# Fifty-four instead of fifty-one pairs of max tiles in front of the loop of a gated attention and token-mixing kernel

## The chip, the core and the metric

The kernel runs on one core of a Trainium2 chip, as one program. The metric is the device time of one execution in microseconds; the median of several runs counts. In the text TensorE multiplies matrices, VectorE and ScalarE work on rows of 128 partitions, GpSimd does elementwise work in on-chip memory, and SyncE issues DMAs.

## The reference

The input x has 2048 tokens of 640 channels. One branch is attention with 32 heads of 20 channels, all of which share one key and one value head; the other is a mixer that applies a two-layer network across the tokens. A sigmoid gate of each token mixes the two.

```python
g = _sigmoid((x * gate_w).sum(-1, keepdims=True))
q = (x @ wq).reshape(B, S, H, Dh); k = x @ wk; v = x @ wv        # S = 2048, H = 32, Dh = 20
p = _softmax(einsum("bhqd,bkd->bhqk", q, k) * Dh ** -0.5)
a = einsum("bhqk,bkd->bhqd", p, v).reshape(B, S, H * Dh) @ wo
h = _layernorm(x)
u = _gelu(einsum("bsd,sf->bdf", h, w1) + b1)                     # F = 1728
y = einsum("bdf,fs->bds", u, w2) + b2
return g * a + (1 - g) * y.transpose(0, 2, 1)
```

## The kernel before

**Units.** Attention is cut into 32 units: four blocks of 512 queries by eight groups of four heads. A unit has 16 key blocks of 128, and in all there are 512 visits (unit, key block). A visit computes four score tiles of 128 keys by 512 queries (`qk`, L685, matmul in L689), ScalarE takes their exponentials (L701), and `pv_mm` (L721, matmul in L724) multiplies them by the values.

**Max tiles.** The softmax needs the largest score of each query before its first exponential. For that every unit has 64 max tiles of its own: a matmul of 128 queries by 512 keys (L507) and a maximum over the row on VectorE (L515). The array is used as two halves of 64 rows, and each half has 32 of the unit's 64 tiles. `ms_next(b)` (L493) gives the next tile of half b, in order through the units; `given[b]` counts those given, so the unit of a half's next tile is `given[b] // 32`. When both halves of a unit are complete, `ms_done` (L524) reduces, negates and splits the maxima; `store_max` and `fetch_max` carry them by DMA into extra rows of the unit's q tile, where the score matmul subtracts them.

**In front of the loop** (L608 to L650) the first ten of 28 blocks of the mixer's first product are computed, 160 steps of six matmuls each (L634). Between steps, `lead()` (L616) issues one pair of max tiles, one in each half of the array; the two run side by side. `LEAD` says how many pairs there are, spread evenly from the fourth step to six before the last (L636). Their results rotate over four banks.

**The loop** (L1240) has 248 stretches, eight to a unit. A stretch has four visits' score tiles of one half of the array, a share of max tiles, and filler matmuls: 72 stretches have 24 of the mixer's first product (L1012), then 128 have 20 or 21 of its second (L839), then 48 have 15 of the attention's output projection (L965). `wants` (L1221) says how many max tiles a stretch gets: 6 in the first two, 10 in the other stretches of the first product, 8 in those of the second. What is left of the 2048 is spread over the output projection's stretches but the last three, in rising order (L1227, L1228). `arrange` (L1158) puts a stretch's instructions in order by a cost table written into the kernel. A last part of eight longer stretches without max tiles ends the program.

**Bursts.** Behind each stretch `burst` (L1189) multiplies the exponentials of an earlier pair of visits by the values: eight products, which follow one another without other matmuls between. If the next stretch's share reaches a unit n whose q tile has been requested, the burst also takes over the waits for q tile n's loads, one on each of its first six products:

```python
        if len(wants) > us[1] // 2 + 2:
            counts = share(us[1] // 2 + 2)
            n = max((given[b] + counts[b] - 1) // 32 for b in range(2))
            if n in qtiles:
                arrived.extend(q_loads.pop(n, ()))
```

**Loads of q.** `new_q(n)` asks for the q tile of unit n as six DMAs of 80 KB from DRAM (L148). Five tiles are alive at a time. It is called behind stretches 8u + 7 (L1252 to L1256): for units 3 and 4 behind stretch 7, 5 and 6 behind stretch 15, and from there on one a unit, u + 5 behind the last stretch of unit u. A load waits until the tile that it overwrites has been read for the last time. SyncE issues all DMAs in program order.

Of the kernel before, what the change touches and what calls it, by code (L numbers as in the profile page):

```python
# [27 lines left out]
NQ = H // 4  # L28
NU = NQB * NQ
PRO = 10  # L30
LEAD = 51
TAIL = 16
FIFTH = (4, 9, 14, 19, 24)
EPS = 1e-5
# [5 lines left out]
def mix_kernel(ctx: ExitStack, tc: tile.TileContext, A_x, A_wq, A_wk, A_wv, A_wo,  # L40
# [567 lines left out]
    with tc.tile_pool(name="psb", bufs=2, space=PSUM, side="right") as psb, \  # L608
# [13 lines left out]
        for fc in range(PRO):  # L622
            pu = [psb.tile([P, NB], F32, name=f"pu{r}") for r in range(2)]
            for hf in range(4):
# [4 lines left out]
                for c in range(HS):  # L629
                    st = hf * HS + c  # L630
                    for k, (w, h) in enumerate(((wh, h_hi[0]), (wh, h_lo[0]), (wl, h_hi[0]))):
                        for r in range(2):
                            rows = slice(64 * r, 64 * r + 64)
                            nc.tensor.matmul(pu[r][:, :HD2], w[rows, c, :], h[rows, st, :],  # L634
                                             start=(st == 0 and k == 0), stop=(st == NS - 1 and k == 2))
                    done = [max(0, min(x, last) - skip) * LEAD // (last - skip) for x in (at, at + 1)]  # L636
                    if done[1] > done[0]:
# [833 lines left out]
```

## Time and profile before

| | |
|---|---|
| median of 3 runs | 1613.25 us (1612.93 to 1613.55) |
| profiled execution | 1613.6 us |
| its span, first to last instruction | 1611.7 us |
| TensorE busy | 1603.9 us |
| VectorE busy | 1378.1 us |
| ScalarE busy | 1262.4 us |
| GpSimd busy | 844.7 us |

A row of the profile names the engine, the line of the kernel and the operation, then the tile that is written and those that are read, the shape, how many there are, and how long one takes. PE stands for TensorE's matmuls, PEld for its weight loads, DVE for VectorE, ACT for ScalarE, POOL for GpSimd, SP for SyncE; a q behind the name stands for the engine's sequencer, which issues DMAs and waits. In a row of the timeline the first number is the start in microseconds from the start of the span and the second the time that the merged group of instructions took; idle time and what ended it stand in brackets. A row of windows has the stretch, its length, the busy time and count of each engine, the granted clock of TensorE, the DMA engines' busy share and the rate in GB/s. A row of waits has the total, the number and the longest in microseconds.

The stage of projections ends at about 96 us, the ten blocks in front of the loop at 179 us; the loop's first product runs until about 614 us, the second until about 1330, the output projection until about 1545.

### The profile page before, as it was taken

The page shows a single profiled execution, that of the slowest core. Times are in us where ns is not written, and L with a number is a line of the kernel's source. Part 1 is how long each engine was busy: PE and PEld are TensorE (multiplying, and loading weights), DVE is VectorE, ACT ScalarE, POOL GpSimd, SP SyncE. Part 2 cuts the span into 40 slices and gives each one's busy share as a digit, 9 for nine tenths or more (in the row PEclk, how much of TensorE's full clock was granted, in tenths as well). Part 3 has the DMA queues.
Part 4 walks back from the last instruction along what each step waited for, and adds up shares of the span by engine and source line. Part 5 has one row for each costly group of instructions (what it writes and reads, how often), then busy time and mean ns, then how long its engine had stood idle before and what let it go on. Part 6 is the DMA issues. An engine that isn't in the chain of part 4 may idle for free.

```text
span 1611.7 us, 39437 instructions
## 1 busy us (share of the span) xinstructions
PE 1603.9 (100%) x14865; PEld 1118.7 (69%) x14865; DVE 1378.1 (86%) x2622; ACT 1262.4 (78%) x2353; POOL 844.7 (52%) x930
## 2 busy tenths in 40 slices
PE   9999999999999999999999999999999999999998
PEld 7899866766767766666666666666666666666665
DVE  6689899999999999888888998888888986667743
ACT  4445677777777778888888888888888889999996
POOL 6567767777787776544554344444444433333340
PEclk9999999999999999999999999999999999999999
DMA  7665322222222122222212121122221113322341
GB/s 216 204 170 140 92 60 75 61 75 76 69 69 76 48 75 63 81 69 69 64 52 59 36 63 57 53 60 61 61 61 47 41 48 102 116 83 82 90 137 57
DMA packets 180437, 129.53 MB, mean 80 GB/s; under 512 B 41617, under 2 KB 150062, under 8 KB 180246
## 3 DMA queue, kind: packets, MB, share of 16 engines
q1 hardware_dynamic: 179958, 126.68, 27.9%
q8 instruction: 117, 1.92, 0.5%
q14 instruction: 74, 0.61, 0.1%
q10 hardware_dynamic: 288, 0.33, 0.1%
HBM read 93.57 MB, written 32.15 MB: 78 GB/s over the span
## 4 chain that ended last, share of the span: by engine, by line
PE 99%; ACT 1%; POOL 0%; DVE 0%; issue 0%; DVEq 0%; POOLq 0%
PE xs L724 30%; PE xs L689 18%; PE xs L507 18%; PE g L839 11%; PE g L1012 7%; PE pp L303 4%; PE pu L634 4%; PE g L965 3%; PE x L507 1%; PE xs L919 1%; PE pp L367 0%; ACT p L701 0%; PE pt L295 0%; PE xs L1436 0%; PE pp L192 0%; PE g L919 0%
## 5 line engine op out<-in xcount | busy, mean ns | idle before, releaser
L515 DVE TENSOR_REDUCE mp<-xs 128x1 f32<-128x512 f32 x1946 | 1198.0, 685 | 146.4 <-PE xs L507 74.8
L701 ACT ACTIVATE p<-xs 128x512 f32<-128x512 f32 (+1 forms) x1840 | 1013.9, 678 | 4.0 <-PE xs L689 2.9
L746 POOL TENSOR_TENSOR osum<-osum,part 128x512 f32<-128x512 f32 x216 | 279.2, 1293 | 615.5 <-ACT part L745 599.1
L724 PE MATMUL xs<-p,v_sb 128*32 128x512 f32 x4096 | 492.3, 598 | 0.0
L689 PE MATMUL xs<-q,kst 62*128 62x512 f32 x1344 | 477.0, 418 | 1.3 <-ACT p L701 1.3
L507 PE MATMUL xs<-kst,q 60*128 60x512 f32 x1242 | 432.8, 415 | 0.0
L689 PEld LDWEIGHTS xs<-q,kst 62*128 62x128 f32 x1344 | 236.6, 185 | 74.8 <-DVE mp L515 53.9
L745 ACT ACTIVATE part<-xs 128x512 f32<-128x512 f32 x216 | 130.0, 602 | 199.7 <-PE xs L724 198.4
L1012 PE MATMUL g<-slot,w 64*128 64x320 f32 x1728 | 266.8, 306 | 0.0
L724 PEld LDWEIGHTS xs<-p,v_sb 128*32 128x32 f32 x4096 | 107.0, 109 | 226.6 <-issue 157.7
L1012 PEld LDWEIGHTS g<-slot,w 64*128 64x128 f32 x1728 | 259.0, 184 | 1.9
L507 PEld LDWEIGHTS xs<-kst,q 60*128 60x128 f32 x1242 | 207.1, 184 | 72.6 <-DVE mp L515 52.0
L127 POOL TENSOR_TENSOR w<-wr,w 128x512 fp32r<-128x512 f32 (+1 forms) x180 | 225.2, 1252 | 34.8 <-ACT w L124 22.7
L689 PE MATMUL xs<-slot,kst 62*128 62x512 f32 x568 | 206.2, 417 | 0.3 <-ACT p L701 0.3
L507 PE MATMUL xs<-kst,slot 60*128 60x512 f32 x576 | 204.4, 418 | 0.0
L839 PE MATMUL g<-u,w 64*128 64x320 f32 x1296 | 201.8, 306 | 0.0
L839 PE MATMUL g<-slot,w 64*128 64x320 f32 x1296 | 201.3, 306 | 0.0
L839 PEld LDWEIGHTS g<-u,w 64*128 64x128 f32 x1296 | 195.7, 184 | 1.5
L839 PEld LDWEIGHTS g<-slot,w 64*128 64x128 f32 x1296 | 195.5, 184 | 1.7
L689 PEld LDWEIGHTS xs<-slot,kst 62*128 62x128 f32 x568 | 99.6, 185 | 30.5 <-DVE mp L515 21.8
L507 PEld LDWEIGHTS xs<-kst,slot 60*128 60x128 f32 x576 | 95.1, 185 | 33.5 <-DVE mp L515 25.2
L965 PE MATMUL g<-slot 64*128 64x320 f32 x720 | 118.2, 306 | 0.0
(189 smaller groups left out, 1448.8 us busy)
## 6 DMA issues: line engine op xcount, KB each, us to landing
wr<-in_B_w_dram SPq DMA_DIRECT2D x155, 256.0 KB
q<-q_scr SPq DMA_DIRECT2D x126, 80.0 KB
rb<-r_scr SPq DMA_DIRECT2D x120, 64.0 KB
slot<-o_scr SPq DMA_DIRECT2D x24, 320.0 KB
y_scr<-yo SPq DMA_DIRECT2D x16, 320.0 KB
q_scr<-qh SPq DMA_DIRECT2D x19, 256.0 KB
q_scr<-ql SPq DMA_DIRECT2D x19, 256.0 KB
o_scr<-rb SPq DMA_DIRECT2D x120, 40.0 KB
```

Of the source, the lines that this page charges most:

```text
L127: nc.gpsimd.tensor_sub(wl, wr, f32(wh))
L303: nc.tensor.matmul(pp, w, t, start=first and n == 0, stop=not more and n == len(steps) - 1)
L507: mm = nc.tensor.matmul(ms, qtiles[n][64 * b:64 * b + 60, pr, qt * P:(qt + 1) * P], kst[64 * b:64 * b + 60, kq * NB:(kq + 1) * NB], start= ...
L515: red = nc.vector.tensor_reduce(out, ms, axis=AX.X, op=ALU.max)
L689: mm = nc.tensor.matmul(s, kst[64 * b:64 * b + 62, kb * P:(kb + 1) * P], q[64 * b:64 * b + 62, pr, :], start=True, stop=True)
L701: act = nc.scalar.activation(p_all[:, a * NB:(j + 1) * NB], s, AF.Exp, scale=SCALE)
L724: mm = nc.tensor.matmul(o[32 * hh:32 * hh + 32, :], v_sb[:, units[u][1], :], p_all[:, j * NB:(j + 1) * NB], start=first, stop=last, skip_g ...
L745: touch(nc.scalar.activation(part, o, AF.Copy), [("x", i)])
L746: nc.gpsimd.tensor_add(osum[n], osum[n], part)
L839: other_tile(half, nc.tensor.matmul(hold["p"][:, :HD2], w[r, fc % HS, :], u[d][r, fc, :], start=(hold["n"] == 1), stop=(hold["n"] == 6 * F ...
L965: other_tile(half, nc.tensor.matmul(hold["p"][:, :HD2], o[r, c, :], w[r, c, d * HD2:(d + 1) * HD2], start=(hold["n"] == 1), stop=(hold["n" ...
L1012: other_tile(half, nc.tensor.matmul(hold["p"][:, :HD2], w[r, st % HS, :], h[d][r, st, :], start=(hold["n"] == 1), stop=(hold["n"] == 6 * NS)))
```

## The change

`LEAD` goes from 51 to 54. `lead()` is called three times more in the same 160 steps, so six max tiles more are done when the loop starts. `wants` gives the output projection's stretches what is left: 204 tiles and not 210. Of its 45 stretches with max tiles, 15 had four and 30 had five; now 21 have four and 24 have five. The share of every other stretch is as before in number; which tiles it holds shifts by three in each half.

```diff
 PRO = 10
-LEAD = 51
+LEAD = 54
 TAIL = 16
```

## The prediction

> **What bounds the kernel now.** I read the page first, then the stages in windows, then single stretches in order of time.
>
> ```profile
> PE 1603.9 (100%) x14865; PEld 1118.7 (69%) x14865; DVE 1378.1 (86%) x2622; ACT 1262.4 (78%) x2353; POOL 844.7 (52%) x930
> ...
> PE 99%; ACT 1%; POOL 0%; DVE 0%; issue 0%; DVEq 0%; POOLq 0%
> ```
>
> ```profile
> core 0: us, PE busy (x) PEld busy (x) DVE busy (x) ACT busy (x) POOL busy (x), PEclk, DMA share, GB/s
> 96.40:179.00 82.60, 82.60 (x1063) 80.27 (x1062) 77.14 (x138) 38.55 (x73) 60.43 (x52) 1.00 0.56 151
> ...
> 189.26:552.64 363.38, 363.38 (x3482) 257.26 (x3481) 361.84 (x684) 286.05 (x527) 258.85 (x306) 1.00 0.26 68
> ...
> 1334.52:1399.31 64.79, 64.79 (x603) 40.37 (x603) 39.62 (x82) 63.22 (x128) 19.77 (x19) 1.00 0.35 105
> 1404.18:1524.93 120.75, 120.75 (x1102) 75.26 (x1101) 85.05 (x171) 112.84 (x226) 40.13 (x38) 1.00 0.30 89
> ```
>
> TensorE has work in every microsecond of every stage, and the chain that ended last runs through it for 99%. So whatever adds TensorE time, or holds up TensorE's queue, lengthens the kernel by that much, unless the engine finds the time again later. The four windows are: the stage in front of the loop; sixty stretches of the first product in the loop; fourteen stretches of the output projection with four max tiles each; twenty-five with five each. In the second window VectorE is busy 361.84 of 363.38 us: there two engines are full at once, and time lost by both can't be found again.
>
> **The three added pairs.** In the stage in front of the loop a pair follows every third step (18 matmuls of L634), now and then every second (12).
>
> ```profile
> 123.96 0.39 PE L507 MATMUL x<-kst,q 60*128 60x512 f32 x2
> 124.19 1.49 PE L634 MATMUL pu<-slot,w 64*128 64x320 f32 x18
> 125.51 0.39 PE L507 MATMUL x<-kst,q 60*128 60x512 f32 x1
> ...
> 174.94 0.39 PE L507 MATMUL x<-kst,q 60*128 60x512 f32 x1
> 175.17 1.05 PE L634 MATMUL pu<-slot,w 64*128 64x320 f32 x12
> 176.06 0.39 PE L507 MATMUL x<-kst,q 60*128 60x512 f32 x2
> ...
> 121.28 1.29 DVE L515 TENSOR_REDUCE mp<-x 128x1 f32<-128x512 f32 x2 [0.27 <-PE x L507]
> ```
>
> From pair to pair it is 125.51 - 123.96 = 1.55 us over three steps and 176.06 - 174.94 = 1.12 us over two. One step is then 0.43 us, and a pair 1.55 - 1.29 = 0.25 us; from the start of a pair to the next L634 it is 124.19 - 123.96 = 0.23. Three pairs cost 3 x 0.235 = **+0.70 us**. Does VectorE follow? Two maxima take 1.29 us with an overlap of 0.09 (one is 0.69), so 1.20 a pair, six tiles 3.6 us more. The 82.60 us window has 77.14 us of it in use, 80.7 after, while the window itself grows to 83.3. There is room, though little, and four banks let the engine lag by a pair; I add nothing. If that cover were gone the price would be bounded by the 3.6 us. The last six pairs stand at the same steps in both kernels, so the passage into the loop is as it was.
>
> **The six tiles that go.** They leave six stretches of the output projection, which change from five max tiles to four. Both kinds are in the trace: 64.79 / 14 = 4.628 us with four and 120.75 / 25 = 4.830 with five. So 6 x 0.202 = **-1.21 us**. Two tiles in front of the loop share one pass of 0.235 us, one each row half; here a tile pays 0.202 alone. That is the whole planned gain: 0.5 us.
>
> **What moves with it.** Between the two places every max tile is computed three tiles per row half earlier, and so is the first use of each unit's q tile, while the loads of q stay where they are: after the stretch in which the unit that held the buffer ends. A burst of products (L724) takes a wait for all six pieces of q(n) if the next stretch's share reaches unit n (L1193). For unit 3: a half has given 51 tiles at the loop's start, then 6 in the first two stretches and 30 in the next six, 87 at the end of stretch 7. Stretch 8 gives its own half 8 more, 95 in all; unit 3 begins with tile 97. So the wait stands a stretch later, in the burst after stretch 8. With 54 the sums are 90 and 98: the wait moves into the burst after stretch 7, and that is the very stretch whose end releases the buffer for q3.
>
> ```profile
> 219.53 1.92 PE L724 MATMUL xs<-p,v_sb 128*32 128x512 f32 x16
> ...
> 225.60 1.92 PE L724 MATMUL xs<-p,v_sb 128*32 128x512 f32 x16
> ...
> 231.67 1.92 PE L724 MATMUL xs<-p,v_sb 128*32 128x512 f32 x16
> ```
>
> ```profile
> SPq L148 <- PE xs L507: 4.5, 1, 4.5
> ```
>
> ```profile
> 224.66 2.21 SPq L148 DMA_DIRECT2D q<-q_scr  x6
> 226.91 2.24 SPq L148 DMA_DIRECT2D w<-q_scr  x6
> ```
>
> ```profile
> 229.27 0.40 SPq L103 DMA_DIRECT2D wr<-in_B_w_dram  x1
> ...
> 229.78 0.44 SPq L103 DMA_DIRECT2D wr<-in_B_w_dram  x1
> ```
>
> ```profile
> L724 PE MATMUL xs<-p,v_sb x20: 592/592/617, 225.6 to 231.7; 128*32 128x512 f32 x20
> ...
> L724 PEldq EVENT_SEMAPHORE  x1: 51/51/51, 231.2 to 231.2; - x1
> ```
>
> The burst after stretch 7 starts at 225.60, the one after stretch 8 at 231.67; the wait stands before the latter (231.2). SyncE had stood 4.5 us for TensorE before it could issue q3, from 224.66 on. When does q3 land? The trace has no row for it, so it is bounded. The issues rotate over eight semaphores, and each waits for the one eight before it: the weight load at 229.27 is eight behind q3's fifth piece, the one at 229.78 eight behind the sixth. So the last piece lands shortly before 229.78; I take 229.7. Today that is 2 us ahead of 231.67 and free. After the change the burst at 225.60 needs it. Its eight products go in two groups of four; the waits hang on the first six, one each, so the sixth, in the second group, waits longest. The second group starts half of (1.92 - 0.59) + 0.22 = 0.89 us into the burst (592 ns is the median of one L724 matmul), at 226.49. The stall is 229.8 - 226.5 = 3.3 us if the first five products slip through while the others wait, and 229.8 - 225.6 = 4.2 if nothing does. One wait alone stands as an instruction of its own (x1), so the others hang on the products themselves, which is nearer to the lower end; I take **+3.5 us**. Behind the waiting product stand the rest of the burst and the whole of stretch 8; VectorE and ScalarE run dry behind it. It isn't found again, since in this stage VectorE has 1.54 us to spare in sixty stretches.
>
> The sixteen loads of units 13 to 28 have their wait one stretch earlier too, in the burst one stretch behind the load's release instead of two. The two tightest by their rows:
>
> ```profile
> 1015.88 2.46 SPq L148 DMA_DIRECT2D q<-q_scr  x6
> ```
>
> ```profile
> 1016.21 1.92 PE L724 MATMUL xs<-p,v_sb 128*32 128x512 f32 x16
> 1021.78 0.64 PE L724 MATMUL xs<-p,v_sb 128*32 128x512 f32 x4
> ```
>
> ```profile
> 1284.55 3.30 SPq L148 DMA_DIRECT2D q<-q_scr  x6
> ```
>
> ```profile
> 1284.86 1.92 PE L724 MATMUL xs<-p,v_sb 128*32 128x512 f32 x16
> 1290.43 1.06 PE L724 MATMUL xs<-p,v_sb 128*32 128x512 f32 x8
> ```
>
> q3's six issues end at 226.87 and its last piece is there by 229.78, 2.9 us later. By the same 2.9 us the later of these two lands at 1287.85 + 2.9 = 1290.8, and the sixth product would come at 1290.43 + 0.89 = 1291.3: 0.5 us to spare. The other lands at 1018.34 + 2.9 = 1021.2 and has until 1022.7: 1.4 us. Between 0 and 0.5 us in all; I take **+0.2**. The row maxima of some units (L537, its split and its store) come a stretch or two earlier, in the same number and beside the same work: nothing.
>
> **Sum.** 0.70 - 1.21 + 3.5 + 0.2 = +3.2 us. The profiled execution took 1613.6 us (span 1611.7, 1.9 around it), 0.35 over the median; 1616.8 for it, so 1616.4 for the median of 1613.25. With the stall from 3.3 to 4.2, the late loads from 0 to 0.5, and half a microsecond off the low end for a last piece that lands well before 229.78, this case by itself spans 1615.6 to 1617.4. A measurement of this kernel can tell some 0.2%, 3.2 us, from no change: the forecast stands right on that edge.
>
> **Rivals.** *The wait costs nothing* (not slower). If q3's pieces were there when the sixth product comes, 0.70 - 1.21 = -0.5 us would be left: 1612.7. For it: the tile itself is read only by the last two max tiles of stretch 8. Against it: the wait is put in front of the burst, and the load can't leave before 224.66, 1.8 us ahead of 226.49, while its issue alone takes 2.21. It decides from a landing before 226.5. 0.07.
>
> *The later loads are late too.* If in eight of them the last piece lands 0.8 us later than I reckon, each stalls 0.3: +2.4 us, 1618.8. For it: 0.5 us of slack at the tightest, and DMA traffic that differs from load to load (2.46 against 3.30 us for the issues alone). Against: the second tightest has 1.4 us by the same reckoning, and all their surroundings shift along. 0.12.
>
> *TensorE's clock falls in the stall.* At the start the clock was half for a while:
>
> ```profile
> 1.45 2.93 PE L192 MATMUL pp<-kst 128*128 128x512 f32 x6 [1.45 <-DVE kst L65]
> 4.17 1.05 PE L295 MATMUL pt<-ident,xa 128*128 128x128 f32 x4
> ...
> 7.33 0.60 PE L295 MATMUL pt<-ident,xa 128*128 128x128 f32 x4
> ```
>
> ```profile
> 186.83 0.49 PE L689 MATMUL xs<-q,kst 62*128 62x512 f32 x1 [0.95 <-ACT p L701]
> ```
>
> Four transposes took 1.05 us at 4.17 and 0.60 at 7.33, so up to 5.9 us of matmuls ran slowly from the first one. The longest pause I found behind that is 0.95 us, with the granted clock at 1.00 in every window above. A stall of 3.5 us is longer; half a clock for 2 to 5.9 us costs 1.0 to 2.9 us, 2.3 as a middle: 1618.7. Against it: TensorE isn't empty all that time, since the first piece, issued 1.9 us before the sixth, lets its product go at about 227.8, which leaves a pause of some 2.2 us behind the 225.6 at which stretch 7 ends. 0.07. [...]
>
> *It doesn't do what it says* can be left aside, since the counts are constants of the program; 0.04 stands for a gain of over 3.2 us from something that I don't see.
>
> **How the numbers follow.** The forecast has 0.70; just under half of it, 0.32, lies above 1616.5. Slower by over 0.2%: 0.32 + 0.12 + 0.07 = 0.51. Within 0.2%: 0.38 + 0.07 = 0.45. Faster: 0.04. The range from 1615.2 to 1619.0 holds the forecast's span, both slower rivals' times, and a margin below; it leaves out the free wait, the gain, and late loads of more than 2.6 us, about 0.2 together.
>
> **What would show it.** In the profile of the changed kernel: the stage in front of the loop 0.7 us longer with pairs at the same pitch; a burst at about 226.3 whose L724 rows spread over 5.3 us and not 1.92, with TensorE idle there until a DMA of q; the burst behind it at about 235.9 and not 231.67; then the same rhythm from burst to burst (6.06, later 5.57 us) with the offset kept; six more stretches of 4.63 us in the output projection. If the offset of about 4.2 us behind stretch 8 is missing, or shrinks before the output projection, the forecast is wrong in that step; if it grows in the middle of the loop, the later loads are late.

## The result and the profile after

| | before | after |
|---|---|---|
| median of 18 runs each, same chip | 1613.26 us (1612.89 to 1614.25) | 1615.84 us (1615.38 to 1616.83) |
| profiled execution, span | 1613.6, 1611.7 us | 1616.83, 1615.0 us |

The change costs 2.58 us; the ratio is 1.0016 with a 95% interval from 1.001 to 1.0022. The profiled execution is the highest of the 18 runs of after, 0.99 us above the median. Most of that lies ahead of any changed code: the first L634 starts at 97.25 us and in before at 96.35; in the experiments' profiles between 95.79 and 96.84. So I compare times between marks inside the kernel, and not the spans.

The page of after first: the engines' busy time, and the chain that ended last.

```profile
PE 1606.8 (99%) x14865; PEld 1119.4 (69%) x14865; DVE 1377.9 (85%) x2622; ACT 1261.8 (78%) x2353; POOL 846.4 (52%) x930
...
PE 97%; DMA 1%; ACT 1%; DVE 0%; SPq 0%; POOL 0%; issue 0%; DVEq 0%
```

The counts are those of before, as they must be, and TensorE is still the chain. In the loop one place stands out. The timelines of TensorE, VectorE and SyncE in after, around the end of stretch 7 (start, duration; in brackets the idle time before and its inferred cause):

```profile
225.87 0.48 PE L507 MATMUL xs<-kst,q 60*128 60x512 f32 x2
227.73 3.93 PE L724 MATMUL xs<-p,v_sb 128*32 128x512 f32 x16 [1.38 <-ACT yo L561]
231.59 0.50 PE L689 MATMUL xs<-q,kst 62*128 62x512 f32 x1
...
235.77 0.64 PE L724 MATMUL xs<-p,v_sb 128*32 128x512 f32 x4
```

```profile
227.44 1.28 DVE L515 TENSOR_REDUCE mp<-xs 128x1 f32<-128x512 f32 x2
232.16 4.89 DVE L515 TENSOR_REDUCE mp<-xs 128x1 f32<-128x512 f32 x8 [3.43 <-PE xs L689]
```

```profile
225.36 2.20 SPq L148 DMA_DIRECT2D q<-q_scr  x6
227.61 2.39 SPq L148 DMA_DIRECT2D w<-q_scr  x6
```

The burst's rows take 3.93 us and not 1.92, behind a pause of 1.38: 1.38 + 3.93 - 1.92 = 3.39 us lost, and VectorE stands empty for 3.43 behind it. Beware of the bracket: it puts the pause down to ScalarE's L561. That is the last event ahead of the burst and not what it waited for: in before the same burst starts at 225.60 and that L561 only at 226.48. The loads of q3 are being issued from 225.36 to 227.56. By the semaphore events in the trace of after the first piece has landed at 227.59 and the sixth at 230.19, and each of the first six products starts 0.04 to 0.14 us behind its piece, the first at 227.73. The second experiment (wait51) puts the same wait in front of the same burst of before, and its timeline names the load for a pause inside the burst.

The stages in the order of time, from the profiled executions; each entry is the time from the mark before it to this one (a burst is its first L724, counted from 1 at the loop's start):

| up to | before | after | difference |
|---|---|---|---|
| first L634 | 96.35 | 97.25 | +0.90 |
| first L689 (stage in front of the loop) | 82.70 | 83.29 | +0.59 |
| burst 1 (the first two stretches) | 10.21 | 9.44 | -0.77 |
| burst 6 | 30.28 | 30.26 | -0.02 |
| burst 8 (the stall) | 12.14 | 15.54 | +3.40 |
| burst 72 (first product) | 387.16 | 387.63 | +0.47 |
| burst 200 (second product) | 715.69 | 715.71 | +0.02 |
| burst 214 | 64.79 | 64.76 | -0.03 |
| burst 221 (six changed stretches and one unchanged) | 33.83 | 32.59 | -1.24 |
| burst 244 | 111.08 | 111.50 | +0.42 |
| end | 67.50 | 67.08 | -0.42 |

Without the start and the last two rows, which move by as much between profiles of kernels with the same number of pairs (burst 221 to 244 took 111.05 to 111.40 us with 51 and 111.12 to 111.56 with 54; the end 66.9 to 67.5 in all of these), the sum is +2.42 us, against 2.58 between the medians.

### The profile page after: what moved, and what is told of

It is laid out like the page before. It is cut to its first block, busy times and chain, and to the rows that moved or that the text cites. A ratio compares the mean times of both kernels' runs of the same rounds, so it can differ in the third digit from the quotient of the medians.

```text
span 1615.0 us, 39430 instructions
## 1 busy us (share of the span) xinstructions
PE 1606.8 (99%) x14865; PEld 1119.4 (69%) x14865; DVE 1377.9 (85%) x2622; ACT 1261.8 (78%) x2353; POOL 846.4 (52%) x930
## 3 DMA queue, kind: packets, MB, share of 16 engines
q8 instruction: 117, 1.92, 0.5%
## 4 chain that ended last, share of the span: by engine, by line
PE 97%; DMA 1%; ACT 1%; DVE 0%; SPq 0%; POOL 0%; issue 0%; DVEq 0%
PE xs L724 30%; PE xs L689 18%; PE xs L507 17%; PE g L839 11%; PE g L1012 7%; PE pu L634 4%; PE pp L303 3%; PE g L965 3%; PE x L507 1%; PE xs L919 1%; ACT p L701 1%; PE pp L367 0%; PE pt L295 0%; DMA xa<-in_A_x_dram 0%; DMA xb<-in_A_x_dram 0%; SPq L188 0%
## 5 line engine op out<-in xcount | busy, mean ns | idle before, releaser
L515 DVE TENSOR_REDUCE mp<-xs 128x1 f32<-128x512 f32 x1940 | 1194.5, 684 | 151.5 <-PE xs L689 82.7
L724 PE MATMUL xs<-p,v_sb 128*32 128x512 f32 x4096 | 494.2, 598 | 1.4 <-ACT yo L561 1.4
L689 PE MATMUL xs<-q,kst 62*128 62x512 f32 x1344 | 476.4, 417 | 0.4 <-ACT p L701 0.3
L689 PEld LDWEIGHTS xs<-q,kst 62*128 62x128 f32 x1344 | 236.8, 185 | 73.1 <-DVE mp L515 51.1
L724 PEld LDWEIGHTS xs<-p,v_sb 128*32 128x32 f32 x4096 | 107.6, 109 | 229.4 <-issue 157.2
L127 POOL TENSOR_TENSOR w<-wr,w 128x512 fp32r<-128x512 f32 (+1 forms) x180 | 226.8, 1262 | 33.3 <-ACT w L124 15.5
L689 PE MATMUL xs<-slot,kst 62*128 62x512 f32 x568 | 205.9, 417 | 0.2 <-ACT p L701 0.2
L689 PEld LDWEIGHTS xs<-slot,kst 62*128 62x128 f32 x568 | 99.8, 185 | 30.8 <-DVE mp L515 21.8
```

The source lines that it names most:

```text
L127: nc.gpsimd.tensor_sub(wl, wr, f32(wh))
L515: red = nc.vector.tensor_reduce(out, ms, axis=AX.X, op=ALU.max)
L689: mm = nc.tensor.matmul(s, kst[64 * b:64 * b + 62, kb * P:(kb + 1) * P], q[64 * b:64 * b + 62, pr, :], start=True, stop=True)
L724: mm = nc.tensor.matmul(o[32 * hh:32 * hh + 32, :], v_sb[:, units[u][1], :], p_all[:, j * NB:(j + 1) * NB], start=first, stop=last, skip_g ...
```

## The experiments

The theory: the wait for q3, moved into the burst after stretch 7, costs 3.4 us, and without it the change would be 0.8 us faster than before. The rival: the loss grows with the number of pairs, without a step. The kernels are named by what they do and by their number of pairs. The first four ran beside before at 1613.36 us, the last four at 1613.22.

**lead52 and lead53: fewer pairs.** With 52 the wait stays where it was in before, with 53 it moves.

```diff
-LEAD = 51
+LEAD = 52        # lead53: 53
```

> LEAD 52. By the wait theory (the loss is one stall at the burst behind stretch 7, and it begins at the count where unit 3 comes into stretch 8's share) nothing is lost here, since the sums are 88 and 96 and unit 3 begins with tile 97: one pair costs 0.235 us, two tiles less in the output projection give 0.40, so 1613.1 us, within 0.8 of it for what the first two stretches do. By the rival (each added pair costs its own time somewhere, 2.58 us over three pairs) it is 0.86 us slower, 1614.1.

> LEAD 53. By the wait theory the sums are 89 and 97, the wait moves into the burst behind stretch 7, and the whole stall of 3.4 us is there at once: 1613.25 + 0.47 - 0.81 + 3.4 = 1616.3 us, or 1615.5 if the first two stretches are 0.8 us shorter as with 54; the burst behind stretch 7 takes 3.9 us. By the rival, two pairs cost two thirds of the loss: 1615.0 us, with no step between 52 and 53.

Measured: 1613.9 us (1.0003, 0.9994 to 1.0012) and 1615.46 (1.0013, 1.0005 to 1.0022). The step of 1.6 us lies between 52 and 53. The rows of the burst after stretch 7, TensorE's timeline, first with 52 pairs and then with 53:

```profile
226.35 1.92 PE L724 MATMUL xs<-p,v_sb 128*32 128x512 f32 x16
```

```profile
226.83 3.60 PE L724 MATMUL xs<-p,v_sb 128*32 128x512 f32 x16 [1.30 <-ACT yo L561]
```

With 52 the burst is the one of before; with 53 it loses 1.30 + 3.60 - 1.92 = 2.98 us (3.04 from burst to burst). lead52 settles less than I wanted: its time lies between what the theory and the rival gave, nearer to the rival's, and half a microsecond over before, though no stall is in its trace. 0.29 of it is found below, under the row maxima. The medians' step is also only half of the stall. Between the marks of the table lead53 has 0.34 us less than lead52 up to burst 72 and 0.37 less up to burst 221; another 0.7 lies behind burst 221, in stretches that are the same in both, and was not followed up. So the two traces tell the theory from the rival here, and the medians alone do not.

**wait51: the wait alone.** Before with its 51 pairs, but the burst behind stretch 7 takes over q3's waits.

```diff
                 n = max((given[b] + counts[b] - 1) // 32 for b in range(2))
+                if us == (12, 13):
+                    n = 3
                 if n in qtiles:
```

> LEAD 51 as before, and the waits for unit 3's q tile put by hand into the burst behind stretch 7. No max tile moves. By the wait theory it loses the stall alone: 1613.25 + 3.4 = 1616.7 us. By the rival nothing changes: 1613.3 us.

Measured: 1616.93 us (1.0022, 1.0013 to 1.003), 3.57 over before. TensorE's timeline:

```profile
226.83 2.06 PE L724 MATMUL xs<-p,v_sb 128*32 128x512 f32 x6 [1.35 <-ACT yo L561]
229.18 1.94 PE L724 MATMUL xs<-p,v_sb 128*32 128x512 f32 x10 [0.29 <-DMA q<-q_scr]
```

The 16 rows are eight products of two rows each. Three products (six rows) start as their pieces land; then comes a pause, for which the profile does name the load of q, and then the rest. The first pause is put down to L561 here too, in a kernel where only the wait differs from before. From burst to burst it is 7.48 + 8.42 - 12.14 = 3.76 us. Why the same wait cost 3.04 us in lead53, 3.40 in after and 3.76 here was not followed up.

**free54: the change without the moved wait.** After, where the burst doesn't take over q3's waits; the two max tiles at the end of stretch 8 that read q3 carry them.

```diff
-                if n in qtiles:
+                if n in qtiles and n != 3:
```

> LEAD 54, and the burst no longer takes over the waits for unit 3's q tile; they stay with the matmuls that read it, the last max tiles of stretch 8 (about 3 us into the stretch, 5 us behind the burst's start, when the load has landed). By the wait theory the 3.4 us come back: 1615.84 - 3.4 = 1612.4 us, 0.8 us faster than before. By the rival it stays near 1615.8.

Measured: 1612.21 us (0.9994, 0.9985 to 1.0003), 3.6 under after, with both stretches back at 6.07. Adding the wait to before costs 3.57, taking it from after gives 3.63: that is shown from both sides.

**lead55 and ask55: one pair more.** With 55 the waits of fifteen later loads move into the burst right behind the stretch that releases the buffer, as that of q3 did with 53; ask55 has the same 55 pairs, but no burst takes over any wait for a load.

```diff
-LEAD = 51
+LEAD = 55
...
-                arrived.extend(q_loads.pop(n, ()))
+                q_loads.pop(n, ())      # ask55 alone
```

> LEAD 55. By the wait theory the counts decide: with 55 the waits of units 13 to 28 come one burst earlier again, into the burst right behind the stretch that releases the buffer, as unit 3's did with 53. By the landings in the profile with 54 (last piece 3.0 to 5.6 us behind that burst's start, unit 14's ahead of it), fifteen of them stall 2.2 to 4.9 us each, 55 us together: about 1671 us, 1655 to 1675. By the rival (a cost of each pair) it is 1616.7 us.

> LEAD 55, and no burst takes over the waits for a q tile; each stays with the max tile that reads it first. By the wait theory that reader stands at the end of the next stretch, some 4.9 us behind the burst's start, where the pieces have landed or lack up to 0.8 us: 0 to 6 us left of the 55, so 1612 to 1618 us. If the price lay in the loads themselves or in the traffic that they meet, it would stay near lead55's time.

Measured: 1670.06 us (1.0362, 1.0343 to 1.038; four runs from 1665.49 to 1675.84) and 1612.61 (0.9995, 0.9986 to 1.0004). In the waits of lead55 TensorE's bursts (L724) stand for loads 15 times, in those of ask55 not once; the answer has the total, the number and the longest:

```profile
PE xs L724 <- DMA q<-q_scr: 20.9, 10, 2.6
PE xs L724 <- DMA slot<-q_scr: 5.8, 5, 1.5
```

So 57 us hang on where the wait stands and not on the loads: the tiles that read them come late enough that hardly any time is lost there. The pauses named are 26.7 us. From burst to burst lead55 is 54 us behind ask55 in their profiles: behind the pauses the products come apart as in the burst after stretch 7 (four of these bursts, at 711.42, 856.49, 1096.53 and 1193.02, take 4.28, 3.37, 4.77 and 4.23 us and not 1.92), and the granted clock was 0.50 in three stretches of 3.41 us (last section). How thin the margin is that the prediction put at 0.5 us for the tightest late load, lead55 doesn't tell, since it moves the waits by a whole stretch, some 5.6 us. The semaphore events of after do: the tightest of the sixteen landed 5.64 us behind the start of the burst at 1289.47, and the product that needs it comes 5.58 + 0.88 = 6.46 behind that, which leaves 0.8 us.

**cast51 and cast54: the entry into the loop.** The first two stretches of after are 0.77 us shorter, which I had not foreseen. Before and after, ScalarE's and GpSimd's timelines, GpSimd's rows first and ScalarE's second in each:

```profile
184.38 0.46 POOL L583 TENSOR_SCALAR yo<-yo 128x320 f32<-128x320 f32 x1
184.92 0.87 POOL L584 TENSOR_TENSOR yo<-yo 128x320 f32<-128x320 f32 x1
...
185.82 0.47 ACT L571 ACTIVATE yo<-yo 128x320 f32<-128x320 f32 x1 [1.25 <-POOL yo L584]
```

```profile
185.09 0.46 POOL L583 TENSOR_SCALAR yo<-yo 128x320 f32<-128x320 f32 x1
185.63 0.87 POOL L584 TENSOR_TENSOR yo<-yo 128x320 f32<-128x320 f32 x1
...
186.54 0.47 ACT L571 ACTIVATE yo<-yo 128x320 f32<-128x320 f32 x1 [0.35 <-POOL yo L584]
```

GpSimd's share of the gelu starts at the same distance from the first L634 (184.38 - 96.35 = 88.03, 185.09 - 97.25 = 87.84), because four weight splits (L126, L127) stand ahead of it. ScalarE's tanh waits for it, the exponentials stand behind the tanh in ScalarE's queue, and TensorE waits for those: the 0.95 us at 186.83, which the prediction quotes. If this is right, time that TensorE spends in front of the loop is hidden behind GpSimd, and GpSimd relieved of part of its splits gives the same gain without any pairs. In all eight kernels with these splits on GpSimd the first burst comes 4.88 to 4.90 us behind the start of L583, and L583 starts 87.84 to 88.45 us behind the first L634, in no order of the pairs. lead53 shows the hiding too: there TensorE waits 0.89 us for a max tile (L515) in front of the first L689, so the stage is 1.40 longer than in before, and the entry 1.21 shorter. cast51 is before with the high halves of four more chunks of weights cast by ScalarE; cast54 is free54 with the same.

```diff
-            if c < 4 * PRO:
+            if c < 4 * PRO + 4:
                 nc.scalar.activation(wh, wr, AF.Copy)
```

> LEAD 51, the last four weight chunks that are split ahead of the loop get their high half from ScalarE (as the ones before them do) and not from GpSimd. Theory: the entry into the loop waits for GpSimd, whose splits delay its part of the last gelu, behind which ScalarE's exponentials queue; the added pairs gave GpSimd time, so their 0.7 us was paid back there. Then this kernel's first two stretches take 9.4 us and not 10.2, and it runs 0.8 us faster: 1612.5. Rival: the 0.8 us come from the banks in which the last pair lies, or by chance; then it stays at 1613.3.

> LEAD 54 with the wait of unit 3's q tile left to its readers (as free54, 1612.2 us) and ScalarE's casts as in cast51. By the theory on GpSimd there is nothing left to gain at the entry: 1612.2 us, first two stretches at 9.4 as in free54, and the three pairs now show at 0.7 us against cast51. By the rival it equals free54 too, but cast51 stays 1.1 us above it instead of 0.3.

Measured: 1612.02 us (0.9991, 0.9982 to 0.9999) and 1611.89 (0.9992, 0.9983 to 1.0001). The entry in windows, from the first L689 to the first burst: before, after, cast51, cast54.

```profile
179.05:189.26 10.21, 8.91 (x79) 7.44 (x77) 7.29 (x13) 8.28 (x16) 9.13 (x12) 1.00 0.37 98
```

```profile
180.53:189.97 9.44, 9.02 (x80) 7.40 (x76) 7.29 (x13) 8.27 (x16) 8.36 (x11) 1.00 0.32 86
```

```profile
178.72:188.10 9.38, 8.73 (x78) 7.42 (x76) 7.12 (x13) 8.68 (x17) 7.30 (x9) 1.00 0.39 109
```

```profile
179.38:188.86 9.48, 8.83 (x80) 7.31 (x77) 7.13 (x13) 8.68 (x17) 6.75 (x9) 1.00 0.31 86
```

And in cast51 ScalarE's tanh has no wait in front of it any more:

```profile
184.62 0.52 ACT L571 ACTIVATE yo<-yo 128x320 f32<-128x320 f32 x1
```

With GpSimd out of the way the entry takes 9.4 us with 51 pairs, and three pairs more now cost what the prediction gave them: from cast51 to cast54 the stage and the entry grow by 0.62 + 0.10 = 0.72 us. The row maxima (see below) add 0.40 and the output projection takes off 1.21, so 0.1 us should be gained, and the medians differ by 0.13. cast54 has the lowest median, 1.3 us under before and 3.95 under after, but only 0.13 under cast51, and its interval touches one: the pairs themselves gain nothing that can be told.

## Why the prediction was right, and where it was not

The forecast was 1616.4 us, the time 1615.84; the loss is 2.58 us, where 3.2 was said. It is inside the 0.2%, at whose edge the forecast stood: the side that was given 0.45 came, and not the one given 0.51. The total came this near partly by luck, since a pass into the loop 0.9 us cheaper than said and row maxima 0.5 us dearer partly cancel. The parts, in the prediction's order:

**The stall of q3: right.** 3.40 us against 3.5. The prediction looked for a burst at about 226.3 whose rows spread over 5.3 us: stretch 7 ends at 225.87 + 0.48 = 226.35, and the burst's last row at 227.73 + 3.93 = 231.66. It took the lower end, by which products slip through as their pieces land, and the first five of after do that. The landing was well bounded: in before the last piece landed at 229.71 by the semaphore events, and 229.7 was said. Burst 8 came at 235.77 (235.9 was said). That the two starts fit so well is luck: the offset of 0.70 that was to come from the three pairs came instead from a start that was 0.90 us later in this profile, less 0.20 for the stage, the entry and the bursts up to the sixth.

**The three pairs: the step that failed.** +0.70 was said, with "the passage into the loop is as it was". The pairs cost +0.59 in the stage, and the passage gave back 0.77: -0.18 together. What was overlooked is the 0.95 us pause at 186.83, quoted in the prediction itself, but for the clock. Followed back one step further, to the 1.25 us that ScalarE waits for GpSimd, it would have told that an engine other than TensorE decides there. cast51 shows it from the other side.

**The output projection: right.** -1.24 against -1.21. The windows from burst 214 to 221 in before and after, six changed stretches and one unchanged:

```profile
1399.31:1433.14 33.83, 33.83 (x309) 21.10 (x308) 23.13 (x47) 31.80 (x64) 10.97 (x12) 1.00 0.36 109
```

```profile
1403.87:1436.46 32.59, 32.59 (x303) 20.35 (x303) 19.81 (x43) 31.86 (x64) 10.96 (x12) 1.00 0.37 115
```

**The later loads: a little too high.** +0.2 was said, +0.02 came over the 128 stretches of the second product, where wait51 and cast51, in which none of these loads moved, differ from before by +0.19 and -0.11. The margin was enough: 0.8 us at the tightest by the semaphore events, where 0.5 was reckoned.

**The row maxima: "nothing" was wrong, by some 0.47 us.** Behind bursts 21, 28, 53 and 60 of after it takes 6.17 to 6.19 us to the next burst, where the same stretches of before take 6.04 to 6.07. In each of the four a row maximum (L537) stands on VectorE directly behind the max tile that completes its unit. VectorE's timeline for unit 4, in before and after:

```profile
323.67 1.28 DVE L515 TENSOR_REDUCE mp<-xs 128x1 f32<-128x512 f32 x2
324.86 0.21 DVE L537 TENSOR_REDUCE mm<-mp 128x16 f32<-128x64 f32 x1
324.99 4.88 DVE L515 TENSOR_REDUCE mp<-xs 128x1 f32<-128x512 f32 x8
```

```profile
315.63 1.28 DVE L515 TENSOR_REDUCE mp<-xs 128x1 f32<-128x512 f32 x2
316.94 0.22 DVE L537 TENSOR_REDUCE mm<-mp 128x16 f32<-128x64 f32 x1
317.08 4.88 DVE L515 TENSOR_REDUCE mp<-xs 128x1 f32<-128x512 f32 x8
```

In before L537 starts 1.19 us behind the start of the two tiles, while the second still runs; in after 1.31 us, when it has ended. It needs that tile's result and doesn't overlap with it in these rows, as it does with a tile that it doesn't need: 0.12 us, in a stage where VectorE is the second full engine (busy for 387.49 of the 387.63 us from burst 8 to burst 72 of after), and four times 0.12 is the 0.47. The counts say where it must happen. A half has given 90 tiles at the end of stretch 7 and 10 more in every two stretches, 2 of them in the stretch that isn't its own, so with 54 pairs a sum ending in 0 or 2 stands at a stretch's end; units 4, 5, 9 and 10 end with tiles 160, 192, 320 and 352. With 51, 53 and 55 the sums end in 7 and 9, 9 and 1, 1 and 3: no unit in this stage ends so, and no such row is in the traces of before, lead53 (-0.05 us) and ask55. With 52 they end in 8 and 0, for units 3, 4, 8 and 9: four such rows are in lead52's trace, and +0.29 us. free54 and cast54 have the four of after, and +0.46 and +0.44. Where such a row stands, the stretch takes 6.12 to 6.19 us in all four kernels. ask55 has +0.44 in this stage without such rows, behind bursts 20, 27, 52 and 59 (6.12 to 6.22 us). That is another matter: these four bursts take over waits for a load of q in lead55, which ask55 leaves to the max tiles, and lead55 has the same tiles there and takes 6.04 to 6.07. A kernel that moves L537 alone wasn't tried; so this cause is read from the traces and not shown by an experiment.

**The clock: right.** The rival was that the stall, longer than the 0.95 us pause of before, would halve the clock. The pause was 1.38 us, and not 2.2: the first piece came sooner than reckoned, and the products behind it spread. A window over the stall in after:

```profile
225.91:229.32 3.41, 2.03 (x11) 0.51 (x8) 2.81 (x6) 1.71 (x4) 1.88 (x2) 1.00 0.47 155
```

The granted clock stayed at 1.00. That it was half at the start of before is read from times alone: six products of 128x512 take 2.93 us from 1.45 on (L192) and 1.64 us from 8.81 on (L367), while the windows of that stretch print 1.00; the trace's first record of the clock begins at 7.21. For how long a stall would halve it, 2 to 5.9 us, was the author's estimate, and the 2 us are shown by no run; the three stretches at 0.50 in lead55 (last section) last 3.41 us each.

**The free wait** and **late loads too** did not come; free54 shows what the free wait would have given, 1612.21, where the rival said 1612.7.

What stays open: the start differs between profiles by up to 1.5 us and the last part by half a microsecond, so no part below that can be read from one profile's ends.

## What to carry to other kernels

When a count shifts where a consumer of a load falls, look first for waits that are taken over early by something else in the queue: here one such wait cost 3.4 us, where the change was to gain 0.5, and with one pair more such waits cost 57 us, while hardly anything was lost where they were left to the consumers themselves. A short pause in the trace of before is worth following back to its first cause even if the change doesn't touch it, since it says which engine decides there, and so whether added work shows. And a reduction that stood directly behind the last of its inputs on the same engine started 0.12 us later here (1.31 us against 1.19), so a shift of a few tiles cost four times 0.12 us.

## What the runs showed of the hardware that I had not expected

In lead55 the granted clock was 0.50 in three stretches, behind pauses of 2.62, 2.48 and 1.88 us, and 1.00 behind one of 2.41 (854.10 to 860.00). Windows of lead55: for each of the three the 3.41 us ahead and the 3.41 us of half clock, and then a pair where nothing happened.

```profile
708.19:711.60 3.41, 0.79 (x8) 0.41 (x6) 2.25 (x5) 1.86 (x4) 2.68 (x3) 1.00 0.39 99
711.60:715.01 3.41, 3.41 (x15) 1.23 (x14) 0.00 (x0) 0.00 (x0) 0.00 (x0) 0.50 0.71 221
1093.89:1097.30 3.41, 0.93 (x6) 0.28 (x4) 1.81 (x5) 1.43 (x3) 2.24 (x3) 1.00 0.49 141
1097.30:1100.71 3.41, 3.41 (x15) 1.25 (x12) 0.00 (x0) 0.00 (x0) 0.00 (x0) 0.50 0.59 196
1189.47:1192.88 3.41, 1.67 (x17) 1.27 (x14) 3.32 (x7) 2.93 (x6) 3.25 (x5) 1.00 0.22 71
1192.88:1196.29 3.41, 3.27 (x14) 1.40 (x16) 0.00 (x0) 0.00 (x0) 0.43 (x1) 0.50 0.70 222
803.76:807.17 3.41, 1.70 (x17) 1.29 (x14) 3.35 (x7) 2.96 (x7) 3.25 (x5) 1.00 0.17 56
807.17:810.58 3.41, 3.14 (x16) 0.94 (x16) 0.00 (x0) 0.00 (x0) 0.45 (x1) 1.00 0.68 225
```

The three starts lie on one grid: 1097.30 - 711.60 = 385.70 is 113 times 3.413, and 1192.88 - 1097.30 = 95.58 is 28 times. In these windows the time that TensorE was busy sorts the cases: those with 0.79, 0.93 and 1.67 us of the 3.41 were followed by one of half clock, the one with 1.70 was not. The length of the pause doesn't sort them, since the one of 1.88 us was followed by half clock and the one of 2.41 was not. One profile with three cases is all there is of this. The stall in after, with its pause of 1.38 us, left 2.03 busy us in the window shown above, more than the 1.70. The pause of 2.2 us that the prediction reckoned with would leave 3.41 - 2.2 = 1.21 us if it fell into one window, less than the 1.67, so the clock could have fallen there: an estimate from these four windows of lead55, which no run tests.
